# A linear-attention layer and an MLP-Mixer block in one kernel: all tasks in another planned order, loads not held back, no zero matmuls in score and output tasks

## Chip, cores and metric

The kernel runs on one core of one Trainium2 chip. The metric is the device time of one execution in microseconds (us). The kernel before was timed in three runs: 164.29, 166.27 and 167.21 us, so the median is 166.27 us.

## What is computed

For each of 4 batches and 8 heads (768 steps, head size 48) a state with a decay is carried through the steps; the 8 heads side by side give rows of 384, and these pass through a token-mixing and a channel-mixing MLP. Cut to what matters:

```
for t in range(S):
    cur = einsum('bhd,bhe->bhde', u * k[t], v[t])
    y[t] = einsum('bhd,bhde->bhe', r[t], state + cur)
    state = w * state + einsum('bhd,bhe->bhde', k[t], v[t])
x = y as (batch, 768, 384)
h = relu(x^T @ w_tok1) @ w_tok2            # 768 -> 256 -> 768
u = x + h^T
out = u + relu(u @ w_ch1) @ w_ch2          # 384 -> 1536 -> 384
```

## The kernel before

**Tiles.** A batch is cut into 6 chunks of 128 steps. For each chunk the keys and receptances are multiplied by powers of the decay (tiles `kr`, from `kt` and `rt` or `win` with the tables `wnat`, `wp`, `wpair`), turned so that the head dimension is on the partitions (`tr_ps`, `trk`, copied to `rka`, `rkb`, `rk`), multiplied to scores (`at_ps`) and masked (`AT`). Scores times values and state times receptances give `y_ps`; `kv_ps` collects the state, kept as `S`. The step's own term (with `u`) is a product `pr` or `rku`, its sum over the head (`ad_ps`, `adg`) and the product `yd` or `ydb` with the values. The chunk's result goes to `x_b`.

When the 6 chunks of a batch are there, the mixer follows: the hidden token rows (`h_ps` from `x_b` and `wtok1`, then `h1r`), back to the steps (`hx_ps` for the first batches, `hT_ps` with a sum `u_sb` for the others), and for each half of the batch (3 chunks, 384 columns) 12 blocks of 128 channels up (`z_ps` from `uT` and `wch1`, three matmuls each, relu to `zr`) and down again (`h_ps` from `zr` and `wch2`), the sum to `osb`, and the store. Matmuls are in bf16 with f32 accumulation. A full-width one is 128x384.

**Order.** Nothing is scheduled at run time. Every piece of work is a task (a load, a turn, 3 to 16 matmuls, one elementwise instruction) that is registered with its dependencies; the list `ORDER` gives the order in which all 910 tasks are recorded, and so the order on every engine. `ENGINES` chooses for each task that two engines could do (0 for the first of its engines, 1 for the second), and `BUFS` chooses the slot of each buffer.

```
    def run(self):
        done = set()
        for n in self.order:
            emit, deps = self.tasks[n]
            assert done.issuperset(deps), n
            self.now = n
            emit()
```

All engines work in this order and wait for each other by semaphores alone. A helper records nearly every operation, so they all have one line, 284, in the profile; tiles are told apart by name.

**Loads.** SP issues all loads of r, k and v (192 KB each; the `win` loads of r for two chunks 384 KB) and nearly all stores, in the planned order. POOL issues the seven weight loads (`wtok`, `wch`), which also change the type from f32 to bf16, between its elementwise work. `W_DEP` lets each weight load wait until a certain input load has landed. `HOLD` does the same between input loads: the fifth to the seventeenth load each wait until an older one has landed.

```
            if (b, c, i) in HOLD:
                after(asked[b, c, i], asked[HOLD[b, c, i]])
```

**Zero matmuls.** 12 tasks of one matmul each on a tile of zeros (`warm`) stand among the first tasks; `FILL` puts 5 more inside score and output tasks of batch 0, through `fill` at the head of `scores`, `outputs` and `add_own`.

```
    def fill(bank, fresh):
        for i in range(FILL.get(plan.now, 0)):
            pe.matmul(bank, warm[:, 0:128], warm[:, 0:bank.shape[-1]], start=fresh, stop=True, skip_group_check=True)
```

Of the kernel before, what the change touches and what calls it, by code (L numbers as in the profile page):

```python
# [63 lines left out]
    0, 1, 2, 0, 1, 0, 2, 1, 0, 2, 1, 0, 2, 1, 0, 1, 2, 1, 0, 2, 1, 0, 2, 0,  # L64
],
    'AT1': [
    0, 1, 2, 0, 1, 0, 2, 1, 0, 2, 0, 1, 2, 1, 0, 1, 2, 1, 0, 1, 2, 0, 1, 2,
],
    'S0': [
    0, 1, 2, 0, 1, 2,  # L70
# [8 lines left out]
    0, 1, 2, 3, 4, 1, 0, 2, 3, 4, 1, 0, 2, 3, 4, 1, 0, 3, 2, 1, 4, 0, 3, 1,  # L79
# [5 lines left out]
    0, 1, 2, 3, 4, 5, 0, 1, 4, 2, 3, 0, 4, 5, 1, 2, 3, 0, 5, 1, 4, 3, 2, 0, 5, 1, 4, 3, 2, 0,  # L85
],
    'kt': [
    0, 1, 2, 3, 4, 5, 0, 1, 2, 3, 4, 5, 0, 1, 2, 3, 4, 5, 0, 1, 2, 3, 5, 4,
],
    'ku': [  # L90
    0, 1, 2, 0, 1, 0, 2, 1, 0, 1, 2, 0,
# [12 lines left out]
],  # L104
    'osb': [
    0, 1, 2, 2, 1, 0, 2, 1, 2, 0, 1, 2, 0, 2, 0, 1, 0, 1, 2, 1, 0, 2, 1, 0, 2,
],
    'pr': [
    0, 1, 1, 0, 1, 0, 1, 0, 1, 0, 1, 0,
],  # L110
    'rk': [
    0, 1, 2, 3, 1, 0, 3, 2, 1, 0, 2, 3,
],
    'rka': [
    0, 1, 2, 0, 1, 2, 0, 1, 2, 0, 2, 1,
],
    'rkb': [
    0, 1, 0, 1, 0, 1,
],
    'rku': [  # L120
    0, 1, 1, 0, 1, 0, 1, 0, 1, 0, 0, 1,
],
    'rt': [
    0, 1, 2, 3, 4, 0, 1, 3, 2, 0, 4, 3,
],
    'uT': [
    0, 1, 2, 3, 0, 1, 3, 2,
],
    'u_sb': [
    0, 1, 2, 3, 0,  # L130
],
    'vb': [
    0, 1, 2, 3, 4, 0, 1, 3, 2, 4, 0, 1, 2, 3, 4, 0, 2, 4, 1, 3, 0, 2, 4, 1,
],
    'vt': [
    0, 1, 2, 3, 4, 5, 0, 1, 3, 2, 4, 5, 0, 3, 1, 2, 4, 5, 0, 3, 1, 2, 4, 5,
],
    'win': [
    0, 1, 2, 1, 0, 2,
],  # L140
    'yd': [
    0, 1, 2, 0, 1, 2, 0, 1, 2, 1, 2, 0, 1, 2, 0, 1, 2, 0,
],
    'ydb': [
    0, 1, 0, 1, 0, 1,
],
    'zr': [
    0, 1, 2, 1, 0, 1, 2, 0,
# [12 lines left out]
]  # L161
W_DEP = [(0, 2, 2), (0, 5, 0), (0, 5, 0), (0, 3, 2), (1, 2, 0), (1, 1, 2), (1, 5, 0)]
HOLD = {(0, 4, 1): (0, 2, 1),
        (0, 1, 2): (0, 0, 0),
        (0, 3, 0): (0, 1, 0),
        (0, 2, 0): (0, 4, 1),
        (0, 4, 0): (0, 1, 2),
        (0, 0, 2): (0, 3, 0),
        (0, 2, 2): (0, 2, 0),
        (0, 3, 2): (0, 4, 0),  # L170
# [1066 lines left out]
```

## Time and profile before

| | |
|---|---|
| timed runs, us | 164.29, 166.27, 167.21 (median 166.27) |
| profiled execution: span from first to last instruction, us | 164.7 |
| mean granted TensorE clock | 0.990 |
| busy us: PE, DVE, POOL, ACT | 155.1, 115.7, 89.4, 65.3 |
| moved by DMA | 26.35 MB, mean 160 GB/s |

The span of the profiled execution lies between the fastest and the median of the timed runs; no other time of that execution is given. PE is TensorE's matmul side and PEld its weight loads, DVE is VectorE, ACT ScalarE, POOL GpSimd, SP the engine that only issues transfers; a q behind a name is the engine's sequencer. "x12" is a count. A busy PE is not PE at its peak: neighbouring matmuls overlap, and a row's mean is the duration of one matmul, not the distance to the next. That distance is read from the chain of work that ended last, where each instruction counts only for the time that it adds.

### The profile page before, as it was taken

How to read it: one execution, taken by the hardware profiler on the slowest of the kernel's cores; microseconds unless marked ns; L12 is line 12 of the kernel's file. 1: busy time of each engine (PE TensorE's matmuls, PEld its weight loads, DVE VectorE, ACT ScalarE, POOL GpSimd, SP SyncE). 2: the span in 40 equal slices, each digit the busy share in tenths (PEclk: the TensorE clock that was granted, in tenths of full speed). 3: DMA queues.
4: the chain of work that ended last, by engine and by line, in shares of the span. 5: the costliest groups of instructions: out<-in, count | busy, mean ns of one | idle time of the engine just before them, and what ended most of it. 6: DMA issues, size and time to landing. Idle time of an engine off the chain costs nothing.

```text
span 164.7 us, 3813 instructions
## 1 busy us (share of the span) xinstructions
PE 155.1 (94%) x1474; PEld 103.8 (63%) x1475; DVE 115.7 (70%) x249; ACT 65.3 (40%) x145; POOL 89.4 (54%) x113
## 2 busy tenths in 40 slices
PE   6997799849999999999999999999999999999992
PEld 1464577525776777677676665677677656766661
DVE  6689894654986499689797968588989273763143
ACT  3989874504572452443407032136840200343000
POOL 7149990117482897999999998959722000000000
PEclk9999999986999999999999999999999999999999
DMA  4999899999989949999998997999640147310042
GB/s 128 196 205 182 142 241 217 208 212 213 206 147 232 174 94 192 233 232 182 187 235 172 202 180 135 209 210 204 138 119 4 48 90 188 113 44 0 0 185 102
DMA packets 90949, 26.35 MB, mean 160 GB/s; under 512 B 85683, under 2 KB 90037, under 8 KB 90933
## 3 DMA queue, kind: packets, MB, share of 16 engines
q1 hardware_dynamic: 88576, 22.88, 66.0%
q0 software_dynamic: 2160, 3.15, 11.2%
q8 instruction: 11, 0.18, 0.5%
q10 hardware_dynamic: 196, 0.11, 0.2%
q14 instruction: 6, 0.04, 0.1%
HBM read 20.46 MB, written 4.72 MB: 153 GB/s over the span
## 4 chain that ended last, share of the span: by engine, by line
PE 77%; DMA 17%; ACT 1%; SPq 1%; issue 1%; DVE 0%
PE h_ps L284 33%; PE z_ps L284 29%; DMA vt<-in_v_dram 12%; DMA kt<-in_k_dram 5%; PE y_ps L284 4%; PE hT_ps L284 3%; PE at_ps L284 3%; PE kv_ps L284 2%; PE tr_ps L284 1%; PE trk L284 1%; PE hx_ps L284 1%; ACT vb L284 1%; SPq L284 1%; ACT rkb L284 0%; PE ad_ps L284 0%
## 5 line engine op out<-in xcount | busy, mean ns | idle before, releaser
L284 PE MATMUL h_ps<-wch,zr 128*128 128x384 bf16 (+1 forms) x300 | 53.9, 320 | 0.0
L284 PE MATMUL z_ps<-uT,wch 128*128 128x384 bf16 x288 | 53.0, 334 | 0.7 <-ACT rka L284 0.7
L284 ACT ACTIVATE zr<-z_ps 128x384 bf16<-128x384 f32 x52 | 24.0, 492 | 48.3 <-PE z_ps L284 46.1
L284 PEld LDWEIGHTS <-wch 128*128 128x128 bf16 x288 | 31.9, 115 | 14.6 <-issue 1.5
L284 PEld LDWEIGHTS <-zr 128*128 128x128 bf16 x300 | 27.3, 98 | 15.1
L284 DVE TENSOR_TENSOR AT<-at_ps,mask 128x512 bf16<-128x512 f32 x48 | 30.6, 684 | 4.2 <-PE at_ps L284 3.9
L284 DVE TENSOR_SCALAR zr<-z_ps 128x384 bf16<-128x384 f32 x44 | 22.9, 551 | 9.0 <-PE z_ps L284 9.0
L284 POOL TENSOR_TENSOR yd<-vb,adg 128x384 f32<-128x384 bf16 x17 | 13.9, 827 | 15.3 <-DVE adg L284 7.3
L284 POOL TENSOR_TENSOR kr<-kt,wnat 128x384 bf16<-128x384 f32 x20 | 20.0, 1002 | 1.0 <-DMA kt<-in_k_dram 0.9
L284 PEld LDWEIGHTS <-kr 128*128 128x128 bf16 x192 | 12.9, 101 | 7.8 <-issue 2.6
L284 DVE TENSOR_TENSOR osb<-u_sb,h_ps 128x384 f32<-128x384 bf16 (+1 forms) x16 | 8.2, 526 | 10.1 <-PE h_ps L284 9.9
L284 DVE TENSOR_TENSOR x_b<-y_ps,yd 128x384 bf16<-128x384 f32 x18 | 9.5, 553 | 4.2 <-PE y_ps L284 4.0
L284 ACT CAST vb<-vt 128x384 bf16<-128x384 f32 x22 | 10.9, 512 | 3.3 <-DMA vt<-in_v_dram 3.1
L284 POOL TENSOR_TENSOR rku<-ku,rt 128x384 f32<-128x384 f32 x12 | 12.0, 999 | 0.2
L284 POOL TENSOR_TENSOR ku<-kt,u_bc 128x384 f32<-128x384 f32 x12 | 12.0, 1000 | 0.0
L284 POOL TENSOR_TENSOR kr<-rt,wp 128x384 bf16<-128x384 f32 x12 | 11.9, 996 | 0.0
L284 DVE TENSOR_TENSOR u_sb<-x_b,hT_ps 128x384 bf16<-128x384 bf16 x15 | 7.7, 550 | 4.5 <-PE hT_ps L284 4.4
L284 PEld LDWEIGHTS <-wtok 128*128 128x128 bf16 x78 | 7.4, 98 | 4.5
L284 POOL TENSOR_TENSOR pr<-rka,rkb 128x512 bf16<-128x512 bf16 x3 | 3.5, 1150 | 11.1 <-ACT rkb L284 7.4
L284 PE MATMUL kv_ps<-vb,kr 128*128 128x96 bf16 x80 | 6.7, 206 | 2.4 <-DVE vb L284 2.4
L284 PE MATMUL h_ps<-x_b,wtok 128*128 128x384 bf16 x48 | 8.8, 326 | 0.0
L284 PE MATMUL y_ps<-vb,AT 128*128 128x48 bf16 x192 | 8.7, 183 | 0.0
(96 smaller groups left out, 182.5 us busy)
## 6 DMA issues: line engine op xcount, KB each, us to landing
kt<-in_k_dram SPq DMA_DIRECT2D x24, 192.0 KB, 3.8
vt<-in_v_dram SPq DMA_DIRECT2D x24, 192.0 KB, 3.8
out_dram<-osb SPq DMA_DIRECT2D x23, 192.0 KB, 2.2
win<-in_r_dram SPq DMA_DIRECT2D x6, 384.0 KB, 5.6
rt<-in_r_dram SPq DMA_DIRECT2D x12, 192.0 KB, 4.2
wch<-in_moe_w_ch_dram POOLq DMA_DIRECT2D x4, 384.0 KB, 6.2
wtok<-in_moe_w_tok_dram POOLq DMA_DIRECT2D x2, 384.0 KB, 6.4
wch<-in_moe_w_ch_dram POOLq DMA_DIRECT2D x1, 768.0 KB, 11.1
```

Source lines behind the costliest of these rows:

```text
L284: return lambda *args, **kw: tc.keep_in_program_order(f(*args, **kw))
```

## The change

Only tables change; no function is edited, and no task is added or removed apart from the 5 matmuls of `FILL`.

```
 ORDER = [
-    0, 3, 22, 54, 18, 6, 16, 8, 898, 42, 59, 21, 899, 43, 39, 23, 53, 7, 13, 24, 19, 9, 2, 14, 56, 1, 11, 17, 4, 900,
+    6, 13, 54, 0, 3, 23, 58, 1, 9, 14, 15, 59, 39, 18, 11, 20, 22, 7, 2, 46, 8, 21, 24, 56, 10, 19, 12, 53, 902, 25,
...
 BUFS = {
     'AT0': [
-    0, 1, 2, 0, 1, 0, 2, 1, 0, 2, 1, 0, 2, 1, 0, 1, 2, 1, 0, 2, 1, 0, 2, 0,
+    0, 1, 2, 1, 2, 1, 0, 2, 1, 0, 2, 1, 0, 2, 1, 0, 2, 1, 1, 0, 2, 0, 1, 0,
...
 ENGINES = [
-    0, 0, 1, 0, 1, 1, 1, 1, 1, 0, 1, 0, 1, 1, 1, 0, 0, 0, 1, 0, 1, 1, 1, 1, 0, 1, 1, 0, 0, 0, 1, 1, 0, 0, 0, 0, 0, 0,
+    1, 0, 0, 0, 1, 0, 0, 1, 1, 0, 1, 0, 0, 1, 0, 0, 1, 0, 1, 0, 0, 1, 1, 1, 0, 1, 1, 1, 1, 0, 1, 0, 0, 0, 0, 0, 0,
...
-HOLD = {(0, 4, 1): (0, 2, 1),
-        (0, 1, 2): (0, 0, 0),
...
-        (1, 0, 0): (0, 5, 0)}
+HOLD = {}
...
-FILL = {138: 2, 154: 1, 159: 1, 190: 1}
+FILL = {}
```

`W_DEP`, the other gates and the 12 separate zero matmuls stay. What moves is shown at three places.

SP's first loads (`win` is r for two chunks, `kt` and `vt` are k and v of one chunk), before:

```order
L284 DMA win<-in_r_dram 128x8x96 x2
L284 DMA kt<-in_k_dram 128x8x48 x2
L284 DMA win<-in_r_dram 128x8x96
L284 DMA vt<-in_v_dram 128x8x48
L284 DMA kt<-in_k_dram 128x8x48 x3
L284 DMA vt<-in_v_dram 128x8x48 x4
L284 DMA kt<-in_k_dram 128x8x48
L284 DMA vt<-in_v_dram 128x8x48
L284 DMA win<-in_r_dram 128x8x96
```

and now:

```order
L275 DMA win<-in_r_dram 128x8x96
L275 DMA kt<-in_k_dram 128x8x48
L275 DMA win<-in_r_dram 128x8x96
L275 DMA kt<-in_k_dram 128x8x48 x3
L275 DMA win<-in_r_dram 128x8x96
L275 DMA vt<-in_v_dram 128x8x48 x2
L275 DMA kt<-in_k_dram 128x8x48 x4
L275 DMA vt<-in_v_dram 128x8x48 x4
L275 DMA win<-in_r_dram 128x8x96 x2
```

Batch 0 needs 18 units of 192 KB (a `win` counts two). Before, they are the first 18; the last row is batch 1's first. Now two `kt` of batch 1 (the last two of the row "kt x4") stand among them, and the last four `vt` of batch 0 come behind these; the last row is two windows of batch 1.

POOL around the first weight loads (`wtok_100`, `wtok_101` and `wch_0` are the weights of the hidden token rows, of the way back and of the first four blocks up), before:

```order
L284 TENSOR_TENSOR kr_68<-kt,wnat_84 128x8x48
L284 TENSOR_TENSOR wGm_95<-bm,wG_92 128x384
L284 TENSOR_TENSOR wGm_94<-bm,wG_91 128x384
L284 DMA wtok_100<-in_moe_w_tok_dram 128x6x256
L284 TENSOR_TENSOR ydb<-vb,adg 128x384 x2
L284 TENSOR_TENSOR kr_71<-kt,wnat_84 128x8x48
L284 DMA wtok_101<-in_moe_w_tok_dram 128x1536
L284 TENSOR_TENSOR ydb<-vb,adg 128x384 x2
L284 DMA wch_0_102<-in_moe_w_ch_dram 128x3x512
L284 DMA wch_1_103<-in_moe_w_ch_dram 128x3x1024
```

and now:

```order
L275 TENSOR_TENSOR kr_70<-kt,wnat_84 128x8x48
L275 TENSOR_TENSOR kr_72<-kt,wnat_84 128x8x48
L275 TENSOR_TENSOR kr_69<-kt,wnat_84 128x8x48
L275 TENSOR_TENSOR ydb<-vb,adg 128x384
L275 TENSOR_TENSOR kr_68<-kt,wnat_84 128x8x48
L275 DMA wtok_100<-in_moe_w_tok_dram 128x6x256
L275 TENSOR_TENSOR ydb<-vb,adg 128x384
L275 TENSOR_TENSOR kr_72<-win,wpair 128x8x48
L275 TENSOR_TENSOR ydb<-vb,adg 128x384
L275 DMA wtok_101<-in_moe_w_tok_dram 128x1536
L275 TENSOR_TENSOR ydb<-vb,adg 128x384
L275 DMA wch_0_102<-in_moe_w_ch_dram 128x3x512
```

The products of chunks 4 and 5 of batch 0 (`kr_70`, `kr_72`) and of chunks 0 and 1 of batch 1 (`kr_69`, `kr_68`) now stand ahead of the first weight load, and a product on batch 1's first window (`kr_72<-win`) ahead of the second.

DVE at the hidden token rows of batch 0, before:

```order
L284 TENSOR_TENSOR S_548<-kv_ps,wGm_94 128x384
L284 TENSOR_TENSOR AT_557<-at_ps,mask 128x512
L284 TENSOR_TENSOR AT_581<-at_ps,mask 128x512
L284 CAST vb<-vt 128x384
L284 TENSOR_TENSOR ydb<-vb,adg 128x384
L284 TENSOR_SCALAR h1r<-h_ps 128x384
L284 TENSOR_TENSOR kr_69<-win,wpair 128x8x48
L284 TENSOR_TENSOR kr_70<-kt,wnat_84 128x8x48
L284 TENSOR_TENSOR kr_69<-win,wpair 128x8x48
```

and now:

```order
L275 TENSOR_TENSOR kr_67<-win,wpair 128x8x48
L275 TENSOR_TENSOR S_0_96<-kv_ps,bm 128x384
L275 COPY adg<-ad_ps 128x8
L275 TENSOR_TENSOR ydb<-vb,adg 128x384
L275 CAST x_b_98<-y_ps 128x384
L275 COPY rka<-trk 128x512
L275 TENSOR_TENSOR pr<-trk,rkb 128x512 x2
L275 CAST vb<-vt 128x384
L275 TENSOR_TENSOR kr_67<-win,wpair 128x8x48
L275 COPY adg<-ad_ps 128x8
L275 TENSOR_SCALAR h1r<-h_ps 128x384
```

Work of batch 1 (`rka`, the two `pr`, `vb`, `kr_67`, the second `adg`), which came behind `h1r` or on other engines before, now stands ahead of it, and the last `x_b` of batch 0 is DVE's own. PE's order moves with these: 334 matmuls now stand ahead of the first one of `z_ps`, 12 of them on zeros, where 291 did before, 17 of them on zeros. At the other end, the last store is a full 384-column one, where it was a half one.

More of the change, by code (lines that the diff above doesn't have):

```diff
@@ L63 @@
     'AT0': [
-    0, 1, 2, 0, 1, 0, 2, 1, 0, 2, 1, 0, 2, 1, 0, 1, 2, 1, 0, 2, 1, 0, 2, 0,
+    0, 1, 2, 1, 2, 1, 0, 2, 1, 0, 2, 1, 0, 2, 1, 0, 2, 1, 1, 0, 2, 0, 1, 0,
 ],
     'AT1': [
-    0, 1, 2, 0, 1, 0, 2, 1, 0, 2, 0, 1, 2, 1, 0, 1, 2, 1, 0, 1, 2, 0, 1, 2,
+    0, 1, 2, 1, 2, 1, 0, 2, 1, 0, 2, 1, 2, 0, 1, 2, 0, 2, 0, 1, 2, 0, 1, 0,
 ],
     'S0': [
-    0, 1, 2, 0, 1, 2,
+    0, 1, 2, 0, 1, 0,
 ],
@@ L78 @@
     'adg': [
-    0, 1, 2, 3, 4, 1, 0, 2, 3, 4, 1, 0, 2, 3, 4, 1, 0, 3, 2, 1, 4, 0, 3, 1,
+    0, 1, 2, 3, 4, 1, 2, 0, 3, 4, 1, 2, 0, 3, 1, 4, 2, 3, 0, 1, 2, 4, 0, 3,
 ],
@@ L84 @@
     'kp': [
-    0, 1, 2, 3, 4, 5, 0, 1, 4, 2, 3, 0, 4, 5, 1, 2, 3, 0, 5, 1, 4, 3, 2, 0, 5, 1, 4, 3, 2, 0,
+    0, 1, 2, 3, 4, 5, 1, 3, 5, 2, 1, 5, 0, 4, 3, 5, 2, 0, 1, 4, 5, 2, 3, 0, 1, 5, 3, 0, 1, 5,
 ],
     'kt': [
-    0, 1, 2, 3, 4, 5, 0, 1, 2, 3, 4, 5, 0, 1, 2, 3, 4, 5, 0, 1, 2, 3, 5, 4,
+    0, 1, 2, 3, 4, 5, 0, 1, 2, 3, 5, 4, 1, 0, 2, 3, 5, 4, 0, 2, 3, 5, 4, 1,
 ],
     'ku': [
-    0, 1, 2, 0, 1, 0, 2, 1, 0, 1, 2, 0,
+    0, 1, 2, 0, 1, 0, 1, 1, 2, 2, 1, 0,
 ],
@@ L96 @@
     'm': [
[7 rows of a table removed]
[8 rows of a table added]
 ],
     'osb': [
-    0, 1, 2, 2, 1, 0, 2, 1, 2, 0, 1, 2, 0, 2, 0, 1, 0, 1, 2, 1, 0, 2, 1, 0, 2,
+    0, 1, 2, 1, 0, 2, 0, 1, 1, 0, 1, 0, 1, 2, 1, 2, 0, 2, 1, 2, 1, 0, 1, 2, 0,
 ],
     'pr': [
-    0, 1, 1, 0, 1, 0, 1, 0, 1, 0, 1, 0,
+    0, 1, 0, 0, 1, 0, 0, 1, 0, 1, 0, 0,
 ],
     'rk': [
-    0, 1, 2, 3, 1, 0, 3, 2, 1, 0, 2, 3,
+    0, 1, 2, 3, 1, 0, 3, 1, 2, 0, 3, 1,
 ],
     'rka': [
-    0, 1, 2, 0, 1, 2, 0, 1, 2, 0, 2, 1,
+    0, 1, 2, 0, 1, 2, 0, 2, 1, 0, 2, 0,
 ],
     'rkb': [
-    0, 1, 0, 1, 0, 1,
+    0, 1, 1, 0, 1, 0,
 ],
     'rku': [
-    0, 1, 1, 0, 1, 0, 1, 0, 1, 0, 0, 1,
+    0, 1, 0, 1, 1, 0, 1, 0, 1, 0, 1, 0,
 ],
     'rt': [
-    0, 1, 2, 3, 4, 0, 1, 3, 2, 0, 4, 3,
+    0, 1, 2, 3, 4, 0, 2, 1, 3, 4, 2, 0,
 ],
@@ L132 @@
     'vb': [
-    0, 1, 2, 3, 4, 0, 1, 3, 2, 4, 0, 1, 2, 3, 4, 0, 2, 4, 1, 3, 0, 2, 4, 1,
+    0, 1, 2, 3, 4, 0, 1, 2, 4, 3, 0, 1, 2, 3, 0, 4, 1, 0, 2, 3, 1, 4, 2, 3,
 ],
     'vt': [
-    0, 1, 2, 3, 4, 5, 0, 1, 3, 2, 4, 5, 0, 3, 1, 2, 4, 5, 0, 3, 1, 2, 4, 5,
+    0, 1, 2, 3, 4, 5, 0, 1, 2, 3, 5, 4, 0, 1, 2, 3, 5, 4, 1, 2, 0, 3, 5, 4,
 ],
@@ L141 @@
     'yd': [
-    0, 1, 2, 0, 1, 2, 0, 1, 2, 1, 2, 0, 1, 2, 0, 1, 2, 0,
+    0, 1, 2, 0, 1, 0, 0, 2, 1, 0, 2, 1, 2, 1, 0, 1, 1, 2,
 ],
@@ L147 @@
     'zr': [
-    0, 1, 2, 1, 0, 1, 2, 0,
+    0, 1, 2, 0, 1, 2, 0, 1,
 ],
@@ L151 @@
 ENGINES = [
[9 rows of a table removed]
[9 rows of a table added]
 ]
 W_DEP = [(0, 2, 2), (0, 5, 0), (0, 5, 0), (0, 3, 2), (1, 2, 0), (1, 1, 2), (1, 5, 0)]
-HOLD = {(0, 4, 1): (0, 2, 1),
-        (0, 1, 2): (0, 0, 0),
[L165 to L170, printed above, removed]
-        (0, 4, 2): (0, 0, 2),
-        (0, 5, 0): (0, 2, 2),
-        (0, 5, 2): (0, 3, 2),
-        (1, 0, 1): (0, 4, 2),
-        (1, 0, 0): (0, 5, 0)}
+HOLD = {}
 GATES = {(2, 0, 2): 1, (2, 4, 1): 3, (3, 1, 0): 2, (3, 1, 1): 6, (3, 5, 2): 5}
```

109 rows, old and new, of tables (BUFS, ENGINES, ORDER) are left out of this document.

## The prediction

> **What bounds the kernel now.** I read the totals and the chain that ended last, then the same chain in order of time, then the stretches.
>
> ```profile
> PE 155.1 (94%) x1474; PEld 103.8 (63%) x1475; DVE 115.7 (70%) x249; ACT 65.3 (40%) x145; POOL 89.4 (54%) x113
> PE 77%; DMA 17%; ACT 1%; SPq 1%; issue 1%; DVE 0%
> ```
>
> PE is the bound over most of the span, and transfers over some 17%. The order of time tells where:
>
> ```profile
> 1.94 5.24 DMA kt<-in_k_dram
> ...
> 14.23 4.02 DMA vt<-in_v_dram
> ...
> 22.38 12.55 DMA vt<-in_v_dram
> ...
> 36.26 3.66 PE z_ps L284 x12
> ...
> 40.12 3.92 PE z_ps L284 x24
> ...
> 151.82 9.79 PE h_ps L284 x72
> ```
>
> Up to 18 us the end hangs on loads, held one behind another; at 22.38 a load of batch 1 (12.55 us) takes over, and the state matmuls of batch 1 wait for it until just after 35. From there to the last matmul at 161.61 the chain is PE alone. Twelve blocks of `z_ps` just behind the wait took 3.66 us, while 24 took 3.92 four us later, so they ran at about half speed.
>
> ```profile
> PE kv_ps L284 <- DVE vb L284: 2.4, 1, 2.4
> 6.20:25.50 19.30, 17.23 (x229) 11.34 (x229) 17.21 (x38) 16.24 (x40) 14.16 (x16) 1.00 1.03 189
> 36.30:40.00 3.70, 3.70 (x21) 1.89 (x20) 1.68 (x5) 0.83 (x3) 1.95 (x3) 0.55 0.93 188
> 40.00:161.65 121.65, 121.60 (x1140) 83.63 (x1136) 87.74 (x175) 41.35 (x93) 68.78 (x75) 1.00 0.72 150
> ```
>
> In the rows of stretches, busy time stands for PE, PEld, DVE, ACT and POOL, then the granted clock, the DMA share and GB/s. The last row is the main one: from 40 us on PE is busy 121.60 of 121.65 us at full clock. No order can shorten that part. What an order can change is **when PE reaches this state, how much it has done by then, and whether it is interrupted later**. The row of 6.2 to 25.5 us shows who is busy meanwhile: DVE, 17.21 of 19.30 us.
>
> So I work out four terms: when the first `z_ps` can start, what PE has done by then, what becomes of the wait and the slow blocks, and the end.
>
> **First `z_ps`.** Before, it came so:
>
> ```profile
> 6.25 1.96 DVE L284 TENSOR_TENSOR kr<-win,wpair 128x384 bf16<-128x384 f32 x4 [1.51 <-DMA win<-in_r_dram]
> 26.33 0.48 ACT L284 CAST x_b<-y_ps 128x384 bf16<-128x384 f32 x1 [0.39 <-PE y_ps L284]
> 27.47 0.56 DVE L284 TENSOR_SCALAR h1r<-h_ps 128x384 bf16<-128x384 f32 x1 [2.00 <-PE h_ps L284]
> 31.47 1.14 PE L284 MATMUL z_ps<-uT,wch 128*128 128x384 bf16 x6 [0.68 <-ACT rka L284]
> 17.20 1.02 POOL L284 DMA_DIRECT2D wtok<-in_moe_w_tok_dram  x1
> 21.00 0.61 POOL L284 DMA_DIRECT2D wtok<-in_moe_w_tok_dram  x1
> 23.40 1.66 POOL L284 DMA_DIRECT2D wch<-in_moe_w_ch_dram  x2
> ```
>
> From `h1r` on DVE to the first `z_ps` are 4.0 us. DVE did 38 instructions from its first product to the last `ydb`. By the new order it does 47 up to the last `x_b`: four more `kr`, a `rkb`, three more of `S` and `x_b`, two memsets and a small product; one `rka` and one `pr` fewer. Prices:
>
> ```profile
> L284 DVE TENSOR_TENSOR kr<-win,wpair 128x384 bf16<-128x384 f32 x8 | 4.8, 627 | 2.1 <-DMA win<-in_r_dram 2.1
> L284 DVE TENSOR_TENSOR S<-kv_ps,wGm 128x384 bf16<-128x384 f32 x6 | 3.3, 550 | 0.4 <-PE kv_ps L284 0.4
> L284 DVE COPY rk<-tr_ps 128x1024 bf16<-128x1024 bf16 x2 | 1.4, 692 | 0.6 <-PE tr_ps L284 0.5
> L284 DVE TENSOR_TENSOR pr<-trk,rkb 128x512 bf16<-128x512 bf16 x9 | 3.7, 418 | 0.4 <-ACT rka L284 0.3
> L284 POOL TENSOR_TENSOR kr<-kt,wnat 128x384 bf16<-128x384 f32 x20 | 20.0, 1002 | 1.0 <-DMA kt<-in_k_dram 0.9
> L284 POOL TENSOR_TENSOR ydb<-vb,adg 128x384 bf16<-128x384 bf16 x4 | 3.3, 834 | 0.4 <-ACT vb L284 0.2 <-ACT adg L284 0.2
> ```
>
> 4 x 0.627 + 0.692 + 3 x 0.550 - 2 x 0.418 (a `rka` is like a `pr`), and about 0.6 for the three small ones, make 4.6 us. Neighbours overlap a little: the four `kr` of the first row took 1.96 us, 0.49 each, not 0.627. I take 0.85 of the sum, 3.9, so DVE has 17.2 + 3.9 = 21.1 us of work. It starts at about 6.0: the first `kr` waits for a load and for its table from ACT, and the load that the first one waited for before was there at 6.25. If it waits as much as before (19.3 - 17.2 = 2.1) and 0.3 more for the turn through PE at the end, the last `x_b` is there at 29.5. It was there at 26.8. Ahead of `h1r` DVE then has a `rka`, two `pr`, `vb`, a `kr` and `adg`: 0.42 + 0.84 + 0.36 + 0.63 + 0.16 = 2.4, by 0.85 about 2.1. So `h1r` starts at 31.6 instead of 27.47, and with 4.0 us behind it `z_ps` starts at 35.6: **4.1 us later**. The lower bound is +1.2: no waiting on DVE (-2.1) and the last 0.8 us before `z_ps` gone, which waited for ACT. The upper one comes from the weights.
>
> **Loads and weights**, which I cost at nothing beside this. A stretch with held loads, one without, and the landing times:
>
> ```profile
> 4.10:16.50 12.40, 11.49 (x100) 6.38 (x100) 9.92 (x29) 11.13 (x24) 6.18 (x8) 1.00 1.03 195
> 24.70:45.30 20.60, 17.42 (x150) 11.63 (x149) 12.58 (x25) 8.20 (x18) 6.36 (x8) 0.92 1.08 211
> wtok<-in_moe_w_tok_dram POOLq DMA_DIRECT2D x2, 384.0 KB, 6.4
> wch<-in_moe_w_ch_dram POOLq DMA_DIRECT2D x4, 384.0 KB, 6.2
> ```
>
> A unit of 192 KB (0.197 MB) takes 1.01 us at 195 GB/s and 0.93 at 211. Letting loads go saves at most 8% of this phase, since the engines' share was already 1.03. The third load, the fifth unit, landed at 1.94 + 5.24 = 7.18. At 0.93 per unit the 14th lands at 15.6, the 20th (batch 0's last) at 21.1, the 22nd (batch 1's first window) at 23.0. The last `vt` of batch 0 came at 18.25 before (14.23 + 4.02), as unit 15; two loads of batch 1 stand ahead of it now. It is due on DVE at some three quarters of 21.1 us, at about 23, so it is hidden, by 2 us.
>
> POOL meets the 14th unit at 15.6. Three `kr`, a `ydb` and a `kr` follow, 4 x 1.0 + 0.83: the first weight load is issued at 20.4 (17.20 before). Issue and `ydb`, 1.7, to 22.1; then the product on the window, which shares the engines with that weight load, from 23.5 to 24.5; `ydb`, and the second weight load goes at 25.3 (21.00 before), landing 6.4 later, at 31.7. `h1r` ends at 32.1, so this is hidden, by 0.4 us only. The third goes at 26.8 and lands at 33.0 by its row, ahead of 35.6; the first lands at 26.8, ahead of 29.5. With POOL 2 us later, `z_ps` moves to 37.2: that is the upper bound, +6.0.
>
> **PE's work done by then.** The 48 further real matmuls are 8 of `tr_ps`, 8 `trk`, 16 `at_ps`, 4 `ad_ps`, 4 `kv_ps` and 8 of `y_ps`.
>
> ```profile
> 44.03 0.45 PE tr_ps L284 x8
> ...
> 45.94 0.45 PE trk L284 x8
> ...
> 49.52 0.17 PE kv_ps L284 x4
> ...
> 50.34 0.55 PE at_ps L284 x16
> ...
> 53.83 0.37 PE y_ps L284 x12
> ...
> 56.77 0.08 PE ad_ps L284 x4
> ```
>
> 0.45 + 0.45 + 0.55 + 0.08 + 0.17 and, of the 0.37, about 0.2 for 8 score matmuls: **1.9 us** less to do behind the first `z_ps`. The 5 zero matmuls of `FILL` count nothing:
>
> ```profile
> L284 PE MATMUL at_ps<-warm 128*128 128x512 bf16 x4 | 1.4, 382 | 0.0
> ```
>
> They ran in the first 18 us, when PE waited for operands anyway. Were they all in the way, taking them out would gain 1.8; were their cover what keeps the clock up, it would lose a slow stretch (below).
>
> **The wait and the slow blocks.** Of the kernel before, 2.4 us of waiting and 3.66 - 1.95 = 1.7 us at half speed lie behind its first `z_ps`, 4.1 together. The load that was waited for is now unit 25, at 25.8 plus the weights' share, some 28 us, long before 35.6. So this wait goes. But PE now waits for DVE from about 29 to 32, in pieces, and can fall to half speed there, and in-order PE has tight operands just behind 35.6. I keep 1.2 of the 4.1 (bounds 0 and 4.1, each cause about a third likely): **2.9 us less**.
>
> The Trainium skill, page "TensorE: Matmul & The Clock Gate", section "HAM oscillation — how this bites in real kernels", says that idle gaps of PE above some 3.4 us bring the half clock. Here one of 2.4 us was followed by the granted clock of 0.55, so the trace does not agree with 3.4 us as a limit. By the rule, pieces of 1 to 2 us would cost nothing, and the forecast would be 0.6 lower; by the row they may.
>
> **The end.** A full last store instead of a half one:
>
> ```profile
> out_dram<-osb SPq DMA_DIRECT2D x23, 192.0 KB, 2.2
> out_dram<-osb SPq DMA_DIRECT2D x1, 96.0 KB, 1.7
> L284 DVE TENSOR_TENSOR osb<-u_sb,h_ps 128x384 f32<-128x384 bf16 x14 | 7.5, 550 | 10.0 <-PE h_ps L284 9.9
> L284 DVE TENSOR_TENSOR osb<-u_sb,h_ps 128x192 f32<-128x192 bf16 x2 | 0.7, 353 | 0.1
> ```
>
> 0.2 for the sum and 0.5 for the landing, at most 0.7; the last store in a quiet queue is quicker than the median, so I take **0.5**.
>
> **Sum.** 4.1 - 1.9 - 2.9 + 0.5 = -0.2. The profiled span 164.7 becomes 164.5. The timed runs' median is 166.27, 1.6 above that span; with the same offset I forecast **166.1 us**: the later start is paid by the wait that goes. From 40 us on I add nothing: DVE is at 87.74 and POOL at 68.78 of 121.65, and the later batches' outputs stand in PE's order about where they stood, save for the first ones of batches 1 and 2, which stand earlier.
>
> **Rivals.**
>
> *Slower: batch 1's first window becomes the gate (chance 0.25).* It is one product in POOL, with two weight loads behind it, and PE's turn of the same window stands ahead of batch 0's last outputs. For it: the margin is 0.4 us, and the load at 22.38 took 12.55 us, three times its neighbours. Against it: that load had two `wch` weights beside it, the window has one. It decides from a landing past 23.9. If loads let go all at once land 4 us later, at 27, the second weight load is at 29.3 and lands at 35.7, and `z_ps` starts at 39.3: 3.7 more, 169.8 us. The page "DMA: Bandwidth & Descriptors", section "Queues, rings and completion order", of the Trainium skill says that each engine takes packets in turn from the queues that have work. By that a longer queue of loads would not hold a weight load up further; no row here shows a weight load with more loads queued, so the chance stays.
>
> *Faster: DVE keeps no waits and no wait is left on PE (chance 0.2).* `z_ps` at 32.7 to 33.5 (+1.6 in the middle) and all 4.1 back: 1.6 - 1.9 - 4.1 + 0.5 = -3.9, 162.4 us. For it: DVE has more work queued that is free of waiting. Against it: it waited 2.1 us in the same phase before, on PE and ACT, whose own order is as tight.
>
> *Clock (chance 0.1).* Without `FILL` and with pieces of waiting PE falls to half speed twice, once before `h1r` and once at `z_ps`: 1.7 + 1.7 - 0.6 = 2.8 more, 168.9 us.
>
> *Loads let go change nothing (within the forecast's 0.45).* SP could be held by a full queue as it was by `HOLD`; at 1.01 per unit the window lands 1.4 later, and `z_ps` 1.0: 167.1.
>
> **How the numbers follow.** About 2% is what a measurement of this kernel can tell from no change: 162.9 to 169.6. The forecast's own range, from its bounds on the start of `z_ps`, is 164 to 168. The range that should hold 8 in 10 reaches to both rivals: 162.4 to 170.0. Faster by over 2%: 0.12, two thirds of the fast rival and nothing else of note, raised to 0.15 for what batch 1's earlier outputs may spare later. Slower: half of the window's case, a third of the clock's and a little for stalls later, 0.20. The rest is 0.65.
>
> **What would show it.** Right: the last `x_b` of batch 0 on DVE near 29.5, `h1r` near 31.6, the first `z_ps` near 35.6, DVE busy above 0.85 from 7 to 29, no load in the chain behind 25 us, weight loads issued near 20.4 and 25.3, PE gapless from 40. Wrong: `z_ps` waiting for a `wch` or `wtok` load, or PE's gaps behind 40 us adding up to over 1 us; then the term at fault is the one that I set to nothing.

## The result, and the profile after

The changed kernel is slower: 172.64 and 172.68 us in two executions; two more took about 180 (the median of all four is 176.26). No trace shows why, and the comparison leaves out, for both kernels, executions more than 1.5% above the kernel's fastest. By the executions that are compared, the ratio to the kernel before is 1.0435, 95% interval 1.0326 to 1.0545. The forecast was 166.1 us, with a range up to 170.0: it missed on the slow side. The profiled execution has a span of 170.6 us (164.7 before) in a time of 172.68.

The page after, its totals and its chain by engine:

```profile
PE 157.3 (92%) x1469; PEld 106.1 (62%) x1470; DVE 126.9 (74%) x263; ACT 60.7 (36%) x132; POOL 86.3 (51%) x108
PE 82%; DVE 13%; DMA 2%; issue 1%; ACTq 0%; DVEq 0%
```

Transfers have left the chain (17% before, 2% now) and DVE has come in, with 13%. Where it comes in is seen in the chain in order of time (start, length, what):

```profile
31.26 0.98 PE h_ps L275 x6
34.76 2.07 PE hx_ps L275 x16
38.18 0.97 PE z_ps L275 x6
...
59.77 0.69 DVE AT L275
60.53 1.10 DVE vb L275
61.73 1.17 DVE yd L275
...
78.98 1.51 DVE zr L275 x3
81.59 1.79 DVE place L275 x2
83.39 1.90 DVE place L275 x2
85.91 1.55 PE z_ps L275 x6
87.46 1.28 PE h_ps L275 x4
...
157.33 9.78 PE h_ps L275 x68
```

Two pieces of DVE stand behind 40 us, where the prediction had PE alone. The larger one is `place`: four small copies that build a constant tile. The stretches and one wait of PE show what they cost (columns as before: busy time of PE, PEld, DVE, ACT, POOL, granted clock, DMA share, GB/s):

```profile
20.00:31.00 11.00, 10.18 (x140) 7.59 (x137) 9.33 (x20) 6.45 (x15) 8.64 (x12) 0.62 1.13 208
36.30:40.00 3.70, 3.70 (x47) 2.61 (x45) 3.39 (x8) 1.55 (x4) 0.00 (x0) 1.00 1.15 215
80.00:86.00 6.00, 3.30 (x31) 2.30 (x30) 5.94 (x11) 2.61 (x6) 6.00 (x8) 1.00 1.22 205
86.00:92.00 6.00, 6.00 (x34) 3.60 (x34) 4.26 (x10) 2.59 (x7) 4.79 (x6) 0.72 1.04 176
40.00:166.90 126.90, 124.05 (x1118) 83.98 (x1116) 93.75 (x184) 40.64 (x90) 67.64 (x73) 0.99 0.71 140
```

```profile
PE z_ps L275 <- DVE zr L275: 2.7, 1, 2.7
```

The first of these stretches in the kernel before, for comparison:

```profile
20.00:31.00 11.00, 10.27 (x143) 7.52 (x142) 7.86 (x17) 6.48 (x19) 4.87 (x7) 1.00 1.22 220
```

From 36.3 to 40 PE now works at full clock (0.55 before): the old wait and its slow blocks are gone. But from 20 to 31 the clock is 0.62 (1.00 before), and from 80 to 92 PE first stands for 2.7 us and then works at 0.72.

**A common measure.** To put all kernels on one scale, I sum the useful matmuls that PE has begun by a time, each at its price at full clock (0.163 us for 384 columns, 0.055 for a turn of 128, 0.034 for a score, 0.043 for `kv` and for the state's outputs, 0.025 for the scores' outputs, from the rows of the prediction). The work is 138.9 us in both kernels. A time minus the work done by then is what PE has **lost** by then; it holds to about 0.3 us:

| us lost by | 30 | 40 | 58 | 66 | 80 | 92 | 158 |
|---|---|---|---|---|---|---|---|
| before | 16.0 | 21.1 | 21.4 | 21.6 | 21.6 | 22.0 | 22.4 |
| changed | 20.7 | 21.5 | 21.8 | 22.7 | 22.7 | 27.2 | 28.0 |

138.9 + 22.4 and 138.9 + 28.0 are 161.3 and 166.9, within 0.3 us of where PE's last matmul ends (161.6 and 167.1); the rest is the last stores. So the 5.9 us of span divide into +0.4 by 40 us, +0.7 from 58 to 66, +4.1 from 80 to 92, +0.4 behind, and +0.3 at the end (3.4 and 3.7). They come from one profile of each kernel, and the kernel before also has executions some 2 to 3 us shorter than its own (experiment 11).

### The profile page after: what moved, and what is told of

Its sections match the earlier page's. It is cut to its first block, busy times and chain, and to the rows that moved or that the text cites. A ratio compares the mean times of both kernels' runs of the same rounds, so it can differ in the third digit from the quotient of the medians.

```text
span 170.6 us, 3779 instructions
## 1 busy us (share of the span) xinstructions
PE 157.3 (92%) x1469; PEld 106.1 (62%) x1470; DVE 126.9 (74%) x263; ACT 60.7 (36%) x132; POOL 86.3 (51%) x108
## 4 chain that ended last, share of the span: by engine, by line
PE 82%; DVE 13%; DMA 2%; issue 1%; ACTq 0%; DVEq 0%
PE h_ps L275 31%; PE z_ps L275 26%; PE y_ps L275 5%; PE at_ps L275 4%; PE kv_ps L275 4%; DVE AT L275 3%; PE hT_ps L275 3%; PE hx_ps L275 3%; PE tr_ps L275 3%; DVE place L275 2%; PE trk L275 2%; DMA wp<-in_w_dram 2%; DVE S L275 1%; DVE zr L275 1%; PE w_ps L275 1%
## 5 line engine op out<-in xcount | busy, mean ns | idle before, releaser
L275 PE MATMUL z_ps<-uT,wch 128*128 128x384 bf16 x288 | 51.4, 330 | 2.7 <-DVE zr L275 2.7
L275 ACT ACTIVATE zr<-z_ps 128x384 bf16<-128x384 f32 x48 | 22.2, 490 | 48.6 <-PE z_ps L275 48.5
L275 DVE TENSOR_TENSOR AT<-at_ps,mask 128x512 bf16<-128x512 f32 x48 | 31.3, 684 | 7.6 <-PE at_ps L275 6.6
L275 DVE TENSOR_SCALAR zr<-z_ps 128x384 bf16<-128x384 f32 x48 | 24.9, 552 | 11.8 <-PE z_ps L275 11.7
L275 PEld LDWEIGHTS <-kr 128*128 128x128 bf16 x192 | 14.2, 111 | 4.7 <-issue 2.4
L275 ACT CAST vb<-vt 128x384 bf16<-128x384 f32 x19 | 9.6, 514 | 0.7 <-DMA vt<-in_v_dram 0.7
L275 PEld LDWEIGHTS <-AT 128*128 128x128 bf16 x192 | 7.7, 100 | 0.5 <-issue 0.3
```

The lines of the kernel that those rows point to most:

```text
L275: return lambda *args, **kw: tc.keep_in_program_order(f(*args, **kw))
```

## The experiments

**Theory.** In the new order the setup of `place` has gone from DVE's first 5 us to 81.4 us, in front of a pair of `zr` whose banks PE needs, and there it is also four times as long; the theory is that each copy has to wait for the POOL product under way. No instruction of the trace reads `place`: the tile serves a path for pairs of chunks, and the table that would choose it (`PAIRED`) is empty in both kernels. The copies before and after (ns: shortest, median, longest; first and last start):

```profile
L284 DVE COPY place<-ident x4: 191/197/226, 3.8 to 4.3; 64x64 bf16<-64x64 bf16 x4
```

```profile
L275 DVE COPY place<-ident x4: 825/994/1049, 81.6 to 84.2; 64x64 bf16<-64x64 bf16 x4
```

One of them with the POOL product beside it:

```profile
83.28 0.99 POOL L275 TENSOR_TENSOR kr<-rt,wp 128x384 bf16<-128x384 f32 x1
83.39 0.94 DVE L275 COPY place<-ident 64x64 bf16<-64x64 bf16 x1
```

The product ends at 84.27 and the copy at 84.33. The other three copies too end some 0.06 us behind a POOL product; the last, at 85.29, behind the one that ends at 85.22.

**Rivals.** `place` only fills a time in which `zr` would have been late anyway; the copies are slow from transfers that crowd that time; the clock that falls in the startup, without the zero matmuls, is the cause; letting loads go is.

**1. `place` early, in the changed kernel.**

```
-... 10, 19, 12, 53, ...   467, 478, 17, 104, ...
+... 10, 19, 12, 17, 53, ...   467, 478, 104, ...
```

> The changed kernel with one number moved: the setup of the tile `place` (a memset and four small copies on DVE) goes from 81.4 us, ahead of a pair of `zr` in the z blocks, to DVE's gap at about 3.5 us. Theory P (the copies stand ahead of `zr`, PE runs out of z banks, idles 2.7 us and then works at half clock): what PE has lost against the kernel before between 82 and 90 us, 4.4 us, goes; span 170.6 - 4.4 = 166.2, time 168.2 us (167.4 to 169.0); no PE wait on `zr` over 0.5 us, PE at 6.0 of 6 us between 80 and 86, clock 1.00 behind it. Rival Z (`place` only stands where DVE would have been late with `zr` anyway, since the new order is tight there): the wait stays above 1.5 us and the time between 171 and 172.7.

Measured: 167.88 us (four executions, 167.37 to 168.04), 4.8 under the 172.66 of the changed kernel; ratio to the kernel before 1.0169 (1.0102 to 1.0235). PE's stretches:

```profile
80.00:86.00 6.00, 6.00 (x52) 4.29 (x50) 4.32 (x10) 3.85 (x10) 6.00 (x8) 1.00 1.37 220
86.00:92.00 6.00, 6.00 (x56) 3.94 (x55) 4.07 (x9) 1.97 (x5) 6.00 (x7) 1.00 0.83 164
```

PE has no gap and full clock where it had 3.30 of 6.00 and 0.72. Lost by 80 and by 92: 22.6 and 22.6. Theory P holds, and Z falls. One number of 910 carried 4.8 of the 6.7 us that lie between 172.66 and 165.98, the median of the kernel before beside it.

**2. `place` where POOL is quiet.** The number 17 goes behind the last `h1r` instead.

> The changed kernel with the setup of `place` moved behind the last `h1r` on DVE, to about 136 us, where POOL has nothing left to do. Theory G (a small bf16 copy within SBUF on DVE waits for the POOL instruction that is under way, so that each copy takes a whole POOL product): the four copies take 0.2 us each here, as at 4 us in the kernel before, against 0.83 to 1.05 at 81 us. Rival L (the copies are slow because the program is late: transfers fill SBUF's ports then): 0.8 us each here too. Time by P and G 168.2 us (167.4 to 169.0), as with the early place; by L up to 1 us more.

```profile
L275 DVE COPY place<-ident x4: 192/200/203, 130.5 to 130.9; 64x64 bf16<-64x64 bf16 x4
```

As short at 130 us as at 4, so the late place in the program alone does not make them slow. POOL's last product has ended at 126.6 us there, but transfers are fewer too; experiment 3 separates the two. Time 167.55 us, ratio 1.0138 (1.0059 to 1.0217).

**3. The copies on ACT,** at their late place.

```
-                dve.tensor_copy(place[rows, j, j::2], ident[rows, rows])
+                act.copy(place[rows, j, j::2], ident[rows, rows])
-    t_place = once("DVE", "place", make_place, [t_id])
+    t_place = once("ACT", "place", make_place, [t_id])
```

> The changed kernel with the setup of `place` left at its late position in the order, its memset on DVE, but its four copies on ACT. Theory G (the copies cost 0.83 to 1.05 us each because DVE and POOL exclude each other on work that reads and writes SBUF only; ACT is not concerned): the four copies take 0.3 us or less each on ACT beside the same POOL products, DVE's `zr` are not held up, PE does not wait for `zr`, and the time is that of the early place, 167.9 us within 0.8. Rival L (SBUF is crowded at that time, by transfers at 200 GB/s): the copies take 0.8 us or more on ACT too, ACT's own three `zr` behind them are late and PE waits 1 us or more; 170 us or more.

```profile
L275 ACT COPY place<-ident x4: 249/261/268, 82.1 to 82.6; 64x64 bf16<-64x64 bf16 x4
```

0.26 us each on ACT, beside the same POOL products and the same transfers. So rival L falls. Time 167.97 us, ratio 1.0183 (1.0107 to 1.0258), as with the early place; PE's waits name a `zr` once, of ACT, 0.3 us.

**4. The converse, in the kernel before:** its number 17 put just ahead of a pair of `zr`.

```
-... 1, 11, 17, 4, 900, ...   466, 604, 557, 462, ...
+... 1, 11, 4, 900, ...   466, 604, 557, 17, 462, ...
```

> The kernel before with one number moved: the setup of `place` goes from 3.6 us to just ahead of the first pair of `zr` behind 80 us, in the z blocks. Theory P and G: four copies of 0.8 to 1.05 us, PE idle 1.5 to 3 us there and half clock for some 3 us behind it; time 166.0 + 3 to 5 = 169.0 to 171.0 us. Rival Z (place is harmless, the new order's other moves did it): 166.0 us within 0.8, no PE wait on `zr` over 0.5 us.

The copies, PE's waits and the stretch:

```profile
L286 DVE COPY place<-ident x4: 491/994/1044, 80.6 to 83.0; 64x64 bf16<-64x64 bf16 x4
```

```profile
PE at_ps L286 <- DVE zr L286: 1.7, 2, 1.4
```

```profile
80.00:92.00 12.00, 10.33 (x110) 7.13 (x109) 11.20 (x21) 4.18 (x11) 11.13 (x13) 1.00 1.04 209
```

Four copies of up to 1.04 us, and 2.3 us lost (22.2 by 80, 24.5 by 88). The time is 168.30 us, ratio 1.0181 (1.008 to 1.0282): slower, and less than expected (169 to 171). PE stood for 1.7 us, within the 1.5 to 3 expected, but the clock stayed at 1.00 behind it, so the expected slow stretch did not come. In the changed kernel PE lost 4.5 us by the same copies: 2.7 by standing, and the rest in the blocks that followed at a clock of 0.72.

**5. The zero matmuls put back,** `place` early.

```
-FILL = {}
+FILL = {138: 2, 154: 1, 159: 1, 190: 1}
```

> The changed kernel with `place` early and the kernel before's five zero matmuls put back into the same four tasks of batch 0. Theory C (without them the clock gate closes in the startup: granted clock 0.62 from 20 to 31 us, where the kernel before had 1.00, and the first `z_ps` is late by what PE's slow turns add to DVE's chain): the clock there is 0.9 or more, the first `z_ps` comes at 36 to 37 us instead of 38.2, and the time is 1 to 2 us under the kernel with only `place` early: 166.2 to 167.2 us. Rival D (DVE's work sets the start, PE's clock does not matter): first `z_ps` at 38.2 within 0.4 us, time as with only `place` early within 0.6 us.

The stretch of 20 to 31, the last `x_b` of batch 0 on DVE, and the first `z_ps` on PE:

```profile
20.00:31.00 11.00, 8.82 (x144) 6.45 (x144) 10.28 (x24) 7.38 (x17) 9.67 (x13) 1.00 1.15 210
```

```profile
29.69 0.56 DVE L275 CAST x_b<-y_ps 128x384 bf16<-128x384 f32 x1 [0.41 <-PE y_ps L275]
```

```profile
36.41 1.14 PE L275 MATMUL z_ps<-uT,wch 128*128 128x384 bf16 x6
```

The clock stays at 1.00, and `z_ps` comes at 36.41 instead of 37.81 (early place alone, whose last `x_b` starts at 31.10): theory C, for the start. But the early start goes with the clock, not with the zero matmuls as such. The profile of experiment 2, which has none of them, shows:

```profile
20.00:31.00 11.00, 8.50 (x136) 6.16 (x135) 10.30 (x24) 7.44 (x17) 9.54 (x13) 1.00 1.19 215
```

```profile
36.50 1.14 PE L275 MATMUL z_ps<-uT,wch 128*128 128x384 bf16 x6
```

Over the eight profiles of the new order, the three with a clock of 1.00 from 20 to 31 have their first `z_ps` at 36.4 to 36.5, and the five with 0.62 to 0.91 have it at 37.0 to 38.3; two of these five have the zero matmuls (experiments 7 and 8).

The time does not follow: 167.99 us, ratio 1.0137 (1.0019 to 1.0254). The profiled execution lost 1.4 us again at 48; whether the others did is not known. There DVE and POOL show:

```profile
46.42 2.50 DVE L275 TENSOR_TENSOR kr<-win,wpair 128x384 bf16<-128x384 f32 x1
48.85 0.41 DVE L275 TENSOR_TENSOR pr<-trk,rkb 128x512 bf16<-128x512 bf16 x1
```

```profile
46.70 1.02 POOL L275 TENSOR_TENSOR kr<-kt,wnat 128x384 bf16<-128x384 f32 x1
47.66 0.83 POOL L275 TENSOR_TENSOR yd<-vb,adg 128x384 f32<-128x384 bf16 x1
```

A product of 0.55 us took 2.50: it ended when both POOL products had. In experiment 6, below, POOL waits for a load at that time, and the same product takes 0.55:

```profile
46.49 0.55 DVE L277 TENSOR_TENSOR kr<-win,wpair 128x384 bf16<-128x384 f32 x1
```

```profile
49.90 0.99 POOL L277 TENSOR_TENSOR kr<-kt,wnat 128x384 bf16<-128x384 f32 x1 [3.38 <-DMA kt<-in_k_dram]
```

This looks like the mechanism of `place` in another spot, and here it comes and goes with the arrival of a load. The profile of experiment 3 has it too: the same product takes 2.13 us there, beside the same two POOL products, and PE waits 1.0 us.

Over all kernels of the new order without the zero matmuls (the changed one and experiments 1 to 3), the mean granted clock of the 14 executions that are compared is 0.960 to 0.996; with them (this one and the next three) it is 0.997 or more in 11 of 15. They help to keep the clock up; they are neither enough for it nor, by the profile of experiment 2, always needed.

**6. One cast more to ACT,** on top of 5.

```
+MOVED = {422: 'ACT'}
         on = list(kinds)[next(self.engines)]
+        on = MOVED.get(len(self.tasks), on)
```

> The changed kernel with `place` early and the five zero matmuls, and one more edit: the cast of batch 1's last `vb`, which took 1.17 us on DVE at 60.4 us beside a POOL product, goes to ACT, idle there for over 5 us. Theory G (DVE work that reads only SBUF waits for POOL's product under way; the cast and the `yd` behind it made PE lose 0.6 to 0.7 us between 58 and 66): PE loses 0.3 us or less there, and the time is 0.3 to 0.5 us under the same kernel without this edit (167.99 us, spans of 164.5 to 166.0): 166.2 to 167.7. Rival O (PE's loss there is its own order: score matmuls wait a turn whatever DVE does): the loss stays 0.6 or more.

Measured: 166.46 us, ratio 1.0192 (1.0102 to 1.0282); the loss from 58 to 66 is 0.5. The cast is gone from DVE, but the `yd` behind it now takes longer:

```profile
58.95 1.37 DVE L277 TENSOR_TENSOR yd<-vb,adg 128x384 f32<-128x384 bf16 x1
```

So it moved the clash more than it removed it. The loss lies between what the two theories expected (0.3 or less, 0.6 or more), and neither is shown.

**7. A product more to POOL,** on top of 6: `MOVED = {403: 'POOL', 422: 'ACT'}`.

> The changed kernel with `place` early, the zero matmuls, the last `vb` of batch 1 on ACT, and a second move of the same kind: the product `kr` on batch 1's third window goes from DVE, where it took 2.50 us beside two POOL products in one run and 0.55 in others, to POOL. Theory G (each move takes away a place where DVE can be held up by POOL): spans of 164.2 to 164.7 in nearly all runs, none near 165.9; median 166.0 to 166.5 us; this would be the best form of the new order, level with the kernel before within 1%. Rival O (the spread between runs comes from elsewhere): spans from 164 to 166 as without this edit.

Measured: 167.39 us, ratio 1.0144 (1.006 to 1.0229), spans of 164.2, 165.3, 165.9 and 166.1. Rival O: the spread stays. In the profiled execution the clock from 20 to 31 was 0.78, with the zero matmuls in place.

**8. Loads held back again,** on top of 5: each of the fifth to seventeenth loads waits for the one three places ahead.

```
-HOLD = {}
+HOLD = {(0, 0, 0): (0, 2, 0),
...
+        (0, 3, 2): (0, 2, 2)}
```

> The changed kernel with `place` early and the zero matmuls, and with the old rule put back: each of the fifth to seventeenth loads waits until the load three places ahead of it has landed. Theory N (letting loads go is worth next to nothing, since the transfers are bound by their rate either way; 8% of a unit at most): first `z_ps` within 0.5 us of 36.4, time within 0.6 us of 167.99. Rival F (loads let go feed DVE and POOL earlier: the first loads landed sooner, 215 GB/s against 196 to 205 in the early slices): with the rule back the first `z_ps` comes 1 to 2 us later, 37.4 to 38.4, and the time is 0.7 to 1.5 us up, 168.7 to 169.5.

Measured: 167.59 us against 167.99, so no loss by the medians. The ratio to the kernel before is 1.0256 (1.0186 to 1.0326), above that of experiment 5, but the two are measured against different executions of the kernel before. The first `z_ps` comes at 37.45, 1.0 later than in 5, but the clock in this profile also fell, to 0.91 from 20 to 31. So the later start can't be put down to the loads.

**9. Loads let go in the kernel before:** `HOLD = {}` alone.

> The kernel before with the loads' waits on older loads taken out, all else as it was. Theory N (next to nothing): time within 0.8 us of 165.8; the wait of PE on `vb` of batch 1 at 33 us, 2.4 us, stays within 1 us of that. Rival F (loads let go come sooner): the load of batch 1 that was waited for lands 2 us or more before 34.9, the wait shrinks under 1 us, and with the slow blocks behind it gone the time is 162 to 164 us.

```profile
PE kv_ps L272 <- DVE vb L272: 2.5, 1, 2.5
```

The wait of 2.4 us is there as before, and the median is 165.66 us beside 165.79 of the kernel before on the same chip; the compared executions give 1.0128 (1.0028 to 1.0227). Theory N: letting loads go gains nothing by itself. What ended the wait in the changed kernel is then most likely where the loads stand in its order; that was not tested alone.

**10. No zero matmuls in the kernel before:** `FILL = {}` alone.

> The kernel before without its five zero matmuls, all else as it was. Theory C (they keep the clock gate open in the startup: in the new order without them three or four of four runs show a mean clock of 0.966 to 0.990, with them none of four): the granted clock falls below 0.9 somewhere between 8 and 31 us in most runs, mean clock 0.96 to 0.98 against 0.99 to 1.00, and the first `z_ps` is 1 to 1.5 us later; time 166.8 to 167.3. Rival D (the new order itself starves PE in the startup, and the zero matmuls mattered only there): clock 1.00 up to 31 us, time within 0.8 us of 165.8.

```profile
8.00:20.00 12.00, 10.86 (x125) 7.86 (x125) 9.80 (x24) 10.81 (x25) 9.17 (x10) 0.72 0.93 177
```

```profile
31.50 1.14 PE L284 MATMUL z_ps<-uT,wch 128*128 128x384 bf16 x6 [0.68 <-ACT rka L284]
```

The clock falls, to 0.72 from 8 to 20 us, and the first `z_ps` still comes at 31.50 (31.47 before). The ratio is 1.0056 (0.9928 to 1.0185): no difference is shown. The profiled execution is the longest of the four (169.47 us), but the other three have a low mean clock as well (0.968 to 0.979). In the old order PE's slow turns of these 12 us were not on the path; in the new one the slow stretch lies later (a clock of 0.61 from 18 to 31 us in the changed kernel), just ahead of the last `x_b`, and costs about 1.5 us of the start. Theory C holds for the clock and fails for the time.

**11. The kernel before once more.**

> The kernel before, unchanged, for a second profile of it: its executions spread from spans of 161.1 to 164.4 us at one granted clock of 0.99 to 1.00, and the profile that the prediction was made from had 164.7. Theory S (what the prediction read as fixed, 2.4 us of waiting on `vb` of batch 1 and the half-speed `z_ps` blocks behind it, is there in some executions only): a profile of 163 us or less has a wait under 1 us or no slow blocks. Rival E (the start is the same in each, the spread comes from waits behind 40 us): PE has lost 20 to 21 us by 40 us in each, and the difference shows after that. Time 165.8 us within 0.8 in any case.

Measured: 166.65 us over ten executions. Its profile has a span of 164.4 us, the wait on `vb` with 2.3, and 20.8 us lost by 40. So it repeats what the prediction read. Of executions with spans of 161 to 163 us, which the kernel before also has, no profile was had: what they spare stays open.

**12. Is the wait of the kernel before free to be had?** Its late load, the first v of batch 1, goes two places up.

```
-... 183, 159, 69, 186, ...   226, 209, 70, 194, ...
+... 183, 159, 70, 69, 186, ...   226, 209, 194, ...
```

> The kernel before with one load moved: batch 1's first load of v, issued at 22.38 us behind two others and landed at 34.93, goes two places up in SP's order, ahead of batch 1's first window, so that it is issued at about 19 us. Theory W (the 2.4 us wait of PE on its `vb` and the slow `z_ps` blocks behind it are a loss that the order alone causes, as the term of the prediction has it): the load lands before 30 us, the wait is under 0.5 us, PE has lost 17 to 18.5 us at 40 us instead of 21.1, and the time is 162.5 to 164 us, which would beat both kernels. Rival T (the transfers of that stretch are full, so another load is late in its place: the `kt` of batch 1 behind it, landed at 28.2): PE waits 1.5 us or more on `kr` or `trk` there, and the time is 165 to 166.5 us.

Measured: 169.73 us, ratio 1.0354 (1.0183 to 1.0525): slower, by an amount that the interval leaves wide. The chain and PE's waits:

```profile
22.07 11.61 DMA kt<-in_k_dram
```

```profile
PE tr_ps L286 <- DVE kr L286: 5.0, 1, 5.0
```

Rival T, at a higher price than it gave. The `kt` that now takes the late load's turn, issued at 22.07 with two `wch` loads behind it, takes 11.61 us (the `vt` before: 12.55, at 22.38), and PE waits 5.0 us for it instead of 2.4 for the other. In both orders one load of that stretch is late.

## Why the prediction was wrong, point by point

**The step that failed: "From 40 us on I add nothing".** The term was put at nothing, and measured 0.7 + 4.1 us and 0.4 more behind, 5.2 of the 5.9. That `place` makes the 4.1 is shown (experiments 1 to 4); for the 0.7 the clash of `vb` and `yd` with POOL is likely, and not shown (experiment 6). The argument was that DVE is at 87.74 of 121.65 us, and so has room. But PE doesn't wait for DVE's share; it waits for the next instruction of an engine that works in order. Four setup copies in front of `zr` are enough, whatever room there is elsewhere. The order showed them there; I had compared the orders only up to the first `z_ps`, and setup tasks I had taken for work of the first microseconds. Had I seen them, a price of 0.2 us each from the row before would still have given under 1 us. Experiment 2 has them at that price, with POOL idle; beside POOL's products they took 0.99. The section on what would make it wrong named this term, and over 1 us of gaps behind 40 us as its sign; the rivals gave it no case of its own.

**The first `z_ps`: 35.6 forecast, 38.02 measured.**

```profile
38.02 1.14 PE L275 MATMUL z_ps<-uT,wch 128*128 128x384 bf16 x6
```

The count of DVE's instructions up to the last `x_b`, 47, was right. With the clock up (experiment 5) that `x_b` is there at 30.25 (29.5 forecast) and `z_ps` comes at 36.41. That the first of these is so near is partly luck: DVE started at 6.7 us (6.0 forecast) and worked 22.4 us (21.1), but waited only 1.2 us (2.4 with the turn through PE). The remaining 1.6 us of the miss go with the clock. In the changed kernel it is 0.62 from 20 to 31, DVE waits 2.4 us, and the last `x_b` is late:

```profile
31.30 0.56 DVE L275 CAST x_b<-y_ps 128x384 bf16<-128x384 f32 x1 [0.41 <-PE y_ps L275]
...
33.74 0.55 DVE L275 TENSOR_SCALAR h1r<-h_ps 128x384 bf16<-128x384 f32 x1
```

I had "The 5 zero matmuls of `FILL` count nothing". For the time of the kernel before no difference is shown (experiment 10); in the new order the slow stretch that mostly comes without them costs about 1.5 us at the start (experiments 1, 2 and 5). The clock rival had one slow stretch before `h1r`, which came, and one at `z_ps`, which didn't.

**The work done by then: 1.9 us,** by the common measure: 14.6 us of work before the first `z_ps`, 16.5 now. Right.

**The wait and the slow blocks: 2.9 us back, of 4.1.** All of it came back: from the first `z_ps` to 58 us PE loses 0.3 us now (21.5 to 21.8), where it lost 4.5 (31.47 - 14.6 = 16.9, to 21.4). So the three terms, forecast as 4.1 - 1.9 - 2.9 = -0.7, were 6.6 - 1.9 - 4.2 = +0.5: two misses, of 2.5 and 1.3 us, that by luck cancelled in part.

**The end: 0.5 forecast, 0.3 to 0.4 measured.** Right within its bounds.

**Two slips of arithmetic.** A `z_ps` at 37.2 is 5.7 us behind 31.47, not 6.0, and the lower bound of +1.2 gives 163.2 us, not 164. Neither touches the forecast itself.

**The rivals.** Batch 1's first window did not become the gate: no wait of PE names a weight load, though the first two were issued at 21.67 and 26.54 us, 1.2 to 1.3 later than forecast. Loads let go changed next to nothing by themselves (experiments 8 and 9), as that part had it.

**What stays open.** Without its `place`, the new order is still 1 to 3% slower than the kernel before by the compared executions (experiments 1, 2 and 5 to 8), though its profiles lose 21.6 to 23.4 us by the end beside 22.4. The clashes with POOL that come and go account for 1.4 us in one profile (experiment 5) and 1.0 in another (experiment 3). The rest hangs on the shorter executions of the kernel before, with spans down to 161.1 us, where the shortest of any form of the new order is 164.2; no profile shows them. Open as well is the reason for the two executions of the changed kernel near 180 us. No form tried here beats the kernel before.

## What to carry to other kernels

When an order is changed, follow every task that leaves its phase, setup ones and dead ones first: on an engine that works in order a task is priced by who waits behind it, not by the engine's share. Take its duration from a row with the same neighbours busy. And try the first suspect by moving it alone, since one number can hold most of a change of hundreds.

## What the runs showed of the hardware

**DVE and POOL exclude each other on some work.** A copy of 64x64 took 0.20 us with POOL idle (at 130 us, experiment 2), 0.99 in the median beside POOL's products, and 0.26 on ACT beside the same products. Not every POOL instruction holds it up: at 4 us in the kernel before, a memset and a select of POOL (0.20 and 0.29 us) overlap the four copies, which still take 0.19 to 0.23. A cast and a product show it too, in the changed kernel:

```profile
60.40 1.00 POOL L275 TENSOR_TENSOR kr<-rt,wp 128x384 bf16<-128x384 f32 x1
60.45 1.17 DVE L275 CAST vb<-vt 128x384 bf16<-128x384 f32 x1
...
61.36 1.12 POOL L275 TENSOR_TENSOR kr<-kt,wnat 128x384 bf16<-128x384 f32 x1
...
61.73 1.17 DVE L275 TENSOR_TENSOR yd<-vb,adg 128x384 f32<-128x384 bf16 x1
...
62.44 1.14 POOL L275 TENSOR_TENSOR yd<-vb,adg 128x384 f32<-128x384 bf16 x1
```

The cast takes 0.35 and the product 0.55 with no POOL product beside them, and POOL's own 1.00 and 0.83 grew to 1.12 and 1.14. A sum over one operand is not touched: `adg` took its 0.55 beside POOL products,

```profile
79.44 1.96 POOL L275 TENSOR_TENSOR kr<-kt,wnat 128x384 bf16<-128x384 f32 x2
...
80.40 0.55 DVE L275 TENSOR_REDUCE adg<-rku 128x8 f32<-128x384 f32 x1
```

and neither is a DVE instruction that reads its main input from PSUM (`x_b` and `zr`, 0.55 throughout). The Trainium skill, page "SBUF — State Buffer", section "Who interferes with whom", has this rule: DVE and GpSimd share one pair of SBUF ports as a lock held for a whole instruction; copies and casts in a two-port mode, and products with two SBUF inputs (against GpSimd work that reads SBUF), take it, while a `tensor_reduce` does not. The rows above agree, but for the memset and the select at 4 us, which held no copy up. It also says that whoever issues first gets the pair. The product of 46.42 us doesn't show that: its row begins 0.28 us ahead of POOL's, yet it ends behind two of them, 0.43 us after the second. The copies' rows, too, end right behind POOL's, so such a row most likely holds the wait as well as the work; in a profile the wait then looks like a long busy row, not like idle time.

**A load beside weight loads.** In two orders the load of batch 1 that was issued ahead of two `wch` loads took 11.61 and 12.55 us, where the median of `vt` is 3.8; which load it was followed from the order. In the changed kernel a `kt` issued at 28.65, ahead of `wch` loads at 28.86 and 31.10, took 12.5 us; there POOL waited for it (7.7 us), and PE did not. That the weight loads are the cause was not tested.
